# Exponentials on GpSimd at both ends of a two-branch attention kernel, and part of a softmax moved from VectorE to GpSimd

## The chip, the core and the metric

The kernel runs on one core of a Trainium2 chip. A core has TensorE (PE in the profile: matrix products into PSUM), ScalarE (ACT: activations), VectorE (DVE) and GpSimd (POOL) for elementwise work, and DMA queues, of which this kernel uses that of SyncE (SP). Each engine runs its own instructions in the order of the program and waits on semaphores for the others. The metric is the time of one execution on the device in microseconds; less is better.

## The reference, cut to what matters

```
x: 2048 x 512 (bf16)
g = sigmoid(sum(x * gate_w, -1))
a = attention of 32 heads of 16 over all 2048 keys, softmax(q k / 4) v, then @ A_wo
b = attention of 32 heads over 8 keys: positions s, s-2, ..., s-14, softmax(q k / 4) v, then @ B_wo
out = g * a + (1 - g) * b
```

Branch A is the full attention: 32 heads x 2048 x 2048 scores, each of which has to go through an exponential. Branch B is the local one: 8 scores for each position and head.

## The kernel before, in words

**Branch A.** The scores are made transposed, in units of 128 keys x 512 queries of one head. There are 2048 such units, in 32 periods of 64 (a period is four heads and one block of 512 queries). One matmul (`ring<-qt,kt_all` or `w<-qt,kt_all`) makes a unit in PSUM, one exponential turns it into a bf16 tile, and one matmul (`acc<-pT,vp_all` or `acc<-pd,vp_all`) multiplies it with the values and adds it to the accumulator of its period. The exponential can be had in two ways:

- on ScalarE, from a ring of PSUM banks, alternately three units and two units at a time (`act_stream`, `act_tail`; tile `pT`, lines `pT<-ring` of 128x1536 and 128x1024). Such a group is called a set below;
- on VectorE, one unit at a time from a PSUM buffer `w` (`dve_unit`): a cubic in the low 16 bits of the score, in four instructions (`ta<-w`, twice `ta<-ta,w`, then `pd<-ta,w`, which writes the bits of a bf16 number). `rider` and `solo` choose the units that take this way, at moments when the recorder below sees a free `w` and a free `pd`.

**Branch B.** It is done in 16 tiles of 128 positions (`b_proj`, `b_attn`), nearly all of it on GpSimd. For each tile GpSimd multiplies the shifted keys with the queries (`prod<-ksh,qb`, 8 instructions in two halves) and adds the products up (`prod<-prod`, `lg<-prod`). VectorE takes the maximum (`mx<-lg`), GpSimd subtracts it (`lg<-lg,mx`), ScalarE takes the exponential (`lg<-lg`), VectorE adds (`ssum<-lg`), takes the reciprocal, and multiplies by it and by 1 - g in one instruction (`lg<-lg,omg,ssum`). Then GpSimd multiplies with the shifted values (`prod<-vsh,lg`, 8 instructions) and adds (`prod<-prod`, `ob<-prod`, `obb<-ob,prod`); TensorE transposes the result (`w<-ident,obb`). Keys and values come through DRAM (`kv_scr`) by DMA into `ksh` (two buffers) and `vsh` (one buffer).

**Other work on GpSimd.** 12 times in the run, three instructions prepare packed queries of branch A (`mq<-qpk`, `mq<-mq,mbias`, `qpk<-mq,qpk`; called a packing job below).

**What sets the order.** The program is recorded by a planner (`Plan`): each piece of work is a generator that yields (engine, priority, duration, function). The planner keeps a clock of each engine, takes the ready piece with the lowest priority, and adds a fixed delay (`LAT`) before what comes next in the same generator. What it records is only an order for each engine; the chip then runs each engine's list in that order, with semaphores where data or buffers are shared. A piece that is late on the chip holds up everything that stands behind its readers on their engines. The planner also writes filler products (`acc<-ident,z`) into idle stretches of TensorE, so that TensorE stays busy.

All instructions go through one helper, so the profile gives nearly all of them the same line (L288); they are told apart by their tiles.

Of the kernel before, what the change touches and what calls it, by code (L numbers as in the profile page):

```python
# [10 lines left out]
ALU = mybir.AluOpType  # L11
# [21 lines left out]
A2 = 128.0 * 0.224337942 / 65536.0 ** 2  # L33
A1 = -128.0 * 0.303542182 / 65536.0
A0 = -128.0 * 0.000107113830


def _ap(base, dims):
# [9 lines left out]
class Plan:  # L48

    LAT = {"pe": 0.17, "act": 0.22, "dve": 0.12, "pool": 0.12, "sp": 0.08}

    def __init__(self, engines):
        self.free = {e: 0.0 for e in engines}
# [186 lines left out]
def kernel(  # L242
# [153 lines left out]
    P.resource("accS", 2)  # L396
    P.resource("kvs", 1)
    P.resource("mq", 1)
    MM = 0.22
    SW = 0.11  # L400
    VP = 0.60
# [4 lines left out]
    QRD = 2  # L406
    SOLO = 1
    TWICE = 0.60
    KRP = 4
    QRP = 3  # L410
    XARR = (5.0, 6.9, 8.8, 10.7)
# [182 lines left out]
    def kb_job(b, prio):  # L594
        for sc in range(NC):
            yield ("wait", ev_kpk[b][sc])
        st = {}
        cn = cneg[:, b, 0:1]
        yield ("dve", prio, 0.08, lambda: V.tensor_reduce(out=cn, in_=kmax_pk[:, b, :], axis=AX.X, op=ALU.max))
        yield ("dve", prio, 0.08, lambda: V.tensor_scalar(out=cn, in0=cn, scalar1=1e-20,  # L600
                                                         scalar2=-(1.0 + 2.0 ** -5), op0=ALU.max, op1=ALU.mult))

        def row():
            st["c"] = work.tile([128, QW], BF16, name="crow", tag="crow", bufs=1)
            V.tensor_copy(out=st["c"][:], in_=_ap(cn, [list(cn.ap[0]), [0, QW]]))
        yield ("dve", prio, VP, row)
        yield ("dve", prio, 0.08, lambda: V.reciprocal(out=cneg[:, b, 1:2], in_=cn))
        yield ("dve", prio, 0.08, lambda: V.tensor_tensor(out=mbias[:, b:b + 1], in0=cneg[:, b, 1:2], in1=m15[:],
                                                         op=ALU.mult))
        yield ("set", ev_kb[b])  # L610
        for sc in range(NC):
            yield ("sp", 0, 0.1, lambda sc=sc: SP.dma_start(out=scr_rows(k_scr[b], S, sc * QW, 1), in_=st["c"][:]))
        yield ("delay", 3.0)
        for g in range(2):
            i = 2 * (b + 1) + g
            yield ("sp", 0, 0.1, lambda i=i, g=g: SP.dma_start(out=kt_all[:, i, :],
                                                               in_=k_scr[b][128 * g:128 * (g + 1), :]))
            yield ("spawn", kt_landed(i))
# [6 lines left out]
    def qpk_job(c_, b, rel, prio):  # L625
        yield ("wait", rel)
        yield ("wait", ev_x[c_])
        yield ("wait", ev_kb[b])
        w = Bank()
        st = {}  # L630

        def pe(s):
            w.open(s, [128, QW])
            for c in range(DC):
                mm(w.t[:], wqr[:, c, 128 * (b + 1):128 * (b + 2)], xT[:, c, c_ * QW:(c_ + 1) * QW],
                   c == 0, c == DC - 1)
        yield ("pe", prio, 4 * MM + SW, pe, "w")

        def lin():
            st["q"] = work.tile([128, 2, QW], BF16, name="qpk", tag="qpk", bufs=2)  # L640
            V.tensor_scalar(out=st["q"][:, 0, :], in0=w.t[:], scalar1=QSC, scalar2=None, op0=ALU.mult)
        yield ("dve", prio, VP, lin)
        yield w.close()
        yield ("spawn", dma_job(lambda: SP.dma_start(out=scr_rows(q_scr[(c_, b)], QW, 0, 0), in_=st["q"][:, 0, :])))

        def relu():
            st["m"] = work.tile([128, QW], FP32, name="mq", tag="mq", bufs=1)
            G.tensor_scalar(out=st["m"][:], in0=st["q"][:, 0, :], scalar1=3.0e38, scalar2=0.0, op0=ALU.min, op1=ALU.max)
        yield ("acq", "mq", prio)
        yield ("pool", -5, 0.80, relu)  # L650
        yield ("pool", -5, 0.80, lambda: G.tensor_scalar(out=st["m"][:], in0=st["m"][:], scalar1=2.0,
                                                         scalar2=mbias[:, b:b + 1], op0=ALU.mult, op1=ALU.add))
        yield ("pool", -5, 1.22, lambda: G.tensor_tensor(out=st["q"][:, 1, :], in0=st["m"][:], in1=st["q"][:, 0, :],
                                                         op=ALU.subtract))
# [124 lines left out]
    DV_MIN = 12  # L779
    DV_END = 7  # L780
    flying = [0]
    njunk = [0]
    held_pv = [[] for _ in range(NP)]

# [52 lines left out]
    def pv_job(p, items, res, prio, act=True):  # L837
# [15 lines left out]
        def f():  # L853
# [17 lines left out]
            for e in list(pdq[p]):  # L871
                if e[0] <= now and (act_left[p] == 0 or cnt[e[2]] < most) and ready(ev_v[(i, e[1])], now):
                    pdq[p].remove(e)
                    cnt[e[2]] += 1
                    todo.append(e[1:4])
                    fin.append(("pd", e[4]))
            if act_left[p] == 0:
                for e in pdq[p]:
                    P.spawn(pv_job(p, [e[1:4]], ("pd", e[4]), 0.9, False), e[0])
                pdq[p].clear()  # L880
            seen = [0] * 4
            order = []
# [35 lines left out]
    def act_stream():  # L918
        while front[0] < NP:
# [32 lines left out]
            def f():  # L952
                shut = acc_open[0]
                twice = (shut is not None and not any(row_left[shut])
                         and P.have(P.now + dur) < TWICE * P.HAM)
                for _ in range(1 + twice):
                    for s_, (p_, t, j) in enumerate(units):
                        qk_mm(ring[:, s_, :], p_, t, j)
                more = MM * twice
                js = [u[2] for u in units]  # L960
                while len(js) < 4:
                    r = rider(js)
                    if r is None:
                        break
                    p_, t, j, s, ds = r
                    js.append(j)
                    wt = wtile(s, [128, QW])
                    qk_mm(wt[:], p_, t, j)
                    P.spawn(dve_unit(p_, t, j, s, ds, wt, ndve[0]), P.now + dur + more + P.LAT["pe"])
                    ndve[0] += 1  # L970
                return float(more)
            yield ("pe", 0, dur, f)
# [14 lines left out]
    def solo(t, end, most=SOLO):  # L987
# [7 lines left out]
        r = rider([], t)  # L995
        if r is None:
            return None
        p_, u, j, s, ds = r
        wt = wtile(s, [128, QW])
        qk_mm(wt[:], p_, u, j)  # L1000
        P.spawn(dve_unit(p_, u, j, s, ds, wt, ndve[0]), t + 0.33 + P.LAT["pe"])
        ndve[0] += 1
        nsolo[0] += 1
        return t
# [2 lines left out]
    def rider(js, now=None):  # L1007
        now = P.now if now is None else now
        for p in (front[0], front[0] + 1):
# [7 lines left out]
            j = max(opts, key=lambda j_: len(pend[p][j_]))  # L1017
            if flying[0] and any(x[6] and x[0] < 4.0 + 0.3 * min(front[0] + UR, 16.3) for x in P.ready["pe"]):
                return None
            if not P.free_at("w", now) or not P.free_at("pd", now):  # L1020
                return None
            act_left[p] -= 1
            act_due[p] -= 1
            flying[0] += 1
            return p, pend[p][j].pop(), j, P.take("w", now), P.take("pd", now)
        return None

    def dve_unit(p, t, j, s, ds, wt, n):
# [23 lines left out]
            yield ("spawn", pv_job(p, [(t, j, st["pd"][:])], ("pd", ds), 0.9, False))  # L1052
        else:
            now = yield ("now",)
            pdq[p].append((now, t, j, st["pd"][:], ds))

    otok_tiles = {}
    oT_tiles = {}
# [200 lines left out]
    def b_attn(t, rel, prio):  # L1259
# [19 lines left out]
        def loadk():  # L1279
            base = kv_scr[16 + t * 128:16 + (t + 1) * 128, :]  # L1280
            st["ksh"] = work.tile([128, W, D], BF16, name="ksh", tag="ksh", bufs=2)
            SP.dma_start(out=st["ksh"][:], in_=_ap(base, [[2 * D, 128], [-DIL * 2 * D, W], [1, D]]))
        yield ("sp", 0, 0.1, loadk)
        yield ("delay", 9.0)

# [52 lines left out]
            st["mx"] = work.tile([128, H], FP32, name="mx", tag="mx", bufs=2)  # L1338
            V.tensor_reduce(out=st["mx"][:], in_=lg[:], axis=AX.X, op=ALU.max)
        yield ("dve", prio, 0.33, mx)  # L1340
        yield ("pool", -4, 0.66, lambda: G.tensor_tensor(out=lg[:], in0=lg[:], in1=bc(st["mx"]), op=ALU.subtract))

        def ex():
            A.activation(out=lg[:], in_=lg[:], func=ACT.Exp)
        yield ("act", -1, 0.4, ex)

        def ssum():
            st["ss"] = work.tile([128, H], FP32, name="ssum", tag="ssum", bufs=2)
# [1 line left out]
        yield ("dve", prio, 0.33, ssum)  # L1350
        yield ("dve", prio, 0.27, lambda: V.reciprocal(out=st["ss"][:], in_=st["ss"][:]))

        def attn():
            V.scalar_tensor_tensor(out=lg[:], in0=lg[:], scalar=omg[:, t:t + 1], in1=bc(st["ss"]), op0=ALU.mult,
                                   op1=ALU.mult)
        yield ("dve", prio, 0.34, attn)
        yield ("delay", 1.0)

        def mul_v(hf, w_):
# [21 lines left out]
        for hf in range(2):  # L1381
# [5 lines left out]
            if hf == 0:  # L1387
                yield ("rel", "prod", 0)
        yield ("rel", "vsh", 0)
        yield ("set", _bmul[t])  # L1390

        def fin1():
# [2 lines left out]
        yield ("pool", gp - 0.5, 1.23, fin1)  # L1395
        yield ("rel", "prod", 0)
        yield ("rel", "ob", 0)
        w2 = Bank()
        cb, tl = t // TPC, t % TPC
        if tl == 0 and cb == 2:  # L1400
# [57 lines left out]
    v_group(0, 4, None, 3)  # L1458
    P.spawn(act_stream())
    P.spawn(g_job(GP))  # L1460
    def due(p):
        return 4.0 + 0.3 * min(p, 2 * NG)

# [32 lines left out]
    if CFG_DEBUG:  # L1496
# [2 lines left out]
        pickle.dump(LOG, open("/tmp/plan.pkl", "wb"))  # L1499
        left = {k: [(y[0], y[3].__name__) for y in v] for k, v in P.ready.items() if v}  # L1500
        left.update({k: [(y[0], y[3].__name__) for y in v] for k, v in P.reqs.items() if v})
        print("plan ends", {e: round(v, 1) for e, v in P.free.items()}, "junk", njunk[0], "dve units", ndve[0], "solo", nsolo[0], "sets", nset[0], left)
        if os.environ.get("PLANONLY"):
            raise SystemExit

# [34 lines left out]
```

## Time and profile before

| | |
|---|---|
| time, median of 5 runs | 880.31 us (877.41 to 881.37) |
| the execution that was profiled | 878.5 us, with a span of 876.7 us |
| ScalarE busy | 842.1 us (96% of the span), 829.7 us of it in 726 sets |
| VectorE busy | 768.1 us (88%), 234 units of branch A |
| TensorE busy | 766.9 us (87%) |
| GpSimd busy | 619.0 us (71%), first product of branch B at 112.2 us, last output at 800.0 us |
| DMA | 59.78 MB, mean 68 GB/s |

All numbers of instructions and durations are of the one profiled execution. In the profile's records two instructions that follow each other on ScalarE, VectorE or GpSimd can overlap by some hundredths or tenths of a microsecond, so the mean of one is a little more than what it adds to a row of them.

### The profile page before, as it was taken

How to read it: one execution, taken by the hardware profiler on the slowest of the kernel's cores; microseconds unless marked ns; L12 is line 12 of the kernel's file. 1: busy time of each engine (PE TensorE's matmuls, PEld its weight loads, DVE VectorE, ACT ScalarE, POOL GpSimd, SP SyncE). 2: the span in 40 equal slices, each digit the busy share in tenths (PEclk: the TensorE clock that was granted, in tenths of full speed). 3: DMA queues.
4: the chain of work that ended last, by engine and by line, in shares of the span. 5: the costliest groups of instructions: out<-in, count | busy, mean ns of one | idle time of the engine just before them, and what ended most of it. 6: DMA issues, size and time to landing. Idle time of an engine off the chain costs nothing.

```text
span 876.7 us, 15956 instructions
## 1 busy us (share of the span) xinstructions
PE 766.9 (87%) x6062; PEld 268.3 (31%) x6062; DVE 768.1 (88%) x1346; ACT 842.1 (96%) x758; POOL 619.0 (71%) x594
## 2 busy tenths in 40 slices
PE   8999989998898888888899999788888988898886
PEld 4332233333223233232333232222232222323222
DVE  4789889988989899989987878998998988989885
ACT  5999999999999999999999999999999999999995
POOL 2000283899797989898898989898989898955000
PEclk9899999999999999999999999999999999989999
DMA  8002213330414230321030403303031330200000
GB/s 289 2 1 96 73 32 116 113 121 22 144 46 146 70 112 19 114 63 46 12 117 30 133 27 119 103 8 108 1 92 43 96 105 7 67 1 7 1 1 25
DMA packets 55709, 59.78 MB, mean 68 GB/s; under 512 B 3648, under 2 KB 52288, under 8 KB 55632
## 3 DMA queue, kind: packets, MB, share of 16 engines
q1 hardware_dynamic: 54816, 58.50, 21.2%
q8 instruction: 47, 0.77, 0.4%
q10 hardware_dynamic: 816, 0.26, 0.1%
q14 instruction: 30, 0.25, 0.1%
HBM read 46.14 MB, written 12.62 MB: 67 GB/s over the span
## 4 chain that ended last, share of the span: by engine, by line
ACT 47%; PE 22%; issue 18%; DVE 12%; DMA 1%; SPq 0%; ACTq 0%
ACT pT L288 46%; PE w L288 8%; PE ring L288 7%; DVE ta L288 6%; PE acc L288 6%; DVE pd L288 1%; DVE lg L288 1%; DMA xr<-in_A_x_dram 1%; DVE accS L288 0%; PE last L288 0%; DVE ssum L288 0%; PE xt L288 0%; ACT lg L288 0%; DVE kvs L288 0%; DVE kpk L288 0%
## 5 line engine op out<-in xcount | busy, mean ns | idle before, releaser
L288 ACT ACTIVATE pT<-ring 128x1536 bf16<-128x1536 f32 x726 | 829.7, 1294 | 17.2 <-PE ring L288 8.4
L288 PE MATMUL ring<-qt,kt_all 32*128 32x512 bf16 x1878 | 293.1, 386 | 87.2 <-ACT pT L288 76.8
L288 DVE SCALAR_TENSOR_TENSOR ta<-ta,w 128x512 f32<-128x512 f32 x468 | 308.8, 681 | 5.0
L288 POOL TENSOR_TENSOR prod<-prod 128x512 f32<-128x512 f32 (+1 forms) x208 | 241.5, 1174 | 6.3
L288 PE MATMUL acc<-pT,vp_all 128*17 128x512 bf16 x1814 | 229.4, 388 | 0.1
L288 PEld LDWEIGHTS <-kt_all 32*128 32x128 bf16 x2112 | 105.0, 91 | 333.4 <-issue 319.0
L288 DVE TENSOR_SCALAR ta<-w 128x512 f32<-128x512 uint16 x234 | 158.1, 685 | 38.6 <-PE w L288 37.6
L288 PE MATMUL acc<-ident,z 128*32 128x512 bf16 (+6 forms) x750 | 168.0, 338 | 6.2 <-DVE accS L288 6.0
L288 DVE SCALAR_TENSOR_TENSOR pd<-ta,w 128x512 uint16<-128x512 f32 x234 | 156.7, 679 | 2.6
L288 POOL TENSOR_TENSOR prod<-ksh,qb 128x512 f32<-128x512 bf16 x128 | 145.6, 1163 | 10.9 <-DVE ta L288 8.8
L288 POOL TENSOR_TENSOR prod<-vsh,lg 128x512 f32<-128x512 bf16 x128 | 136.6, 1098 | 10.2 <-DVE lg L288 7.9
L288 PE MATMUL w<-qt,kt_all 32*128 32x512 bf16 x234 | 87.5, 387 | 1.2 <-DVE osb L288 0.6
L288 POOL TENSOR_SCALAR mq<-qpk 128x512 f32<-128x512 bf16 x12 | 7.4, 613 | 106.8 <-DVE qpk L288 106.8
L288 PE MATMUL acc<-pd,vp_all 128*17 128x512 bf16 x234 | 80.1, 386 | 0.2
L288 PEld LDWEIGHTS <-z 128*32 128x32 bf16 x774 | 51.7, 95 | 81.4 <-issue 63.5
L288 PEld LDWEIGHTS <-vp_all 128*17 128x17 bf16 x2048 | 44.5, 88 | 89.0 <-issue 86.5
L288 PE MATMUL w<-bw,xT 128*128 128x512 bf16 x192 | 49.6, 381 | 3.3 <-DVE pd L288 1.6
L288 PEld LDWEIGHTS <-xT 128*128 128x128 bf16 x512 | 31.4, 97 | 37.5 <-issue 24.0
L288 POOL TENSOR_TENSOR lg<-lg,mx 128x256 f32<-128x256 f32 x16 | 10.1, 629 | 37.2 <-DVE mx L288 37.1
L288 DVE CAST kvs<-w 128x512 bf16<-128x512 f32 x32 | 22.0, 687 | 11.7 <-PE w L288 11.6
L288 DVE COPY accS<-acc 128x512 f32<-128x512 f32 (+1 forms) x32 | 21.6, 675 | 1.8 <-ACT accS L288 1.5
L288 POOL TENSOR_TENSOR obb<-ob,prod 128x512 bf16<-128x512 f32 x16 | 20.3, 1271 | 1.3
(110 smaller groups left out, 438.5 us busy)
## 6 DMA issues: line engine op xcount, KB each, us to landing
ksh<-kv_scr SPq DMA_DIRECT2D x16, 1024.0 KB
vsh<-kv_scr SPq DMA_DIRECT2D x16, 1024.0 KB
kv_scr<-kvs SPq DMA_DIRECT2D x16, 256.0 KB
kt_all<-k_scr SPq DMA_DIRECT2D x6, 512.0 KB
q_scr<-qpk SPq DMA_DIRECT2D x24, 128.0 KB
qt<-q_scr SPq DMA_DIRECT2D x24, 128.0 KB
xr<-in_A_x_dram SPq DMA_DIRECT2D x4, 512.0 KB
out_dram<-osb SPq DMA_DIRECT2D x14, 128.0 KB
```

Of the source, the lines that this page charges most:

```text
L288: return chain_on(self._key, f(*a, **k))
```

## The change

- A third way to the exponential, on GpSimd (`pool_unit`): VectorE copies a unit's scores from PSUM into an SBUF tile `psc` (fp32, two buffers), and GpSimd does the cubic there, rewritten so that it takes six instructions with plain operands (three with one tensor operand, three with two). `psc` also holds the two intermediate tiles, and it lies in the buffer of `vsh`. So units go to GpSimd only before branch B begins (`ev_lent`) and after its last tile. The result, and the release of `psc`, are read 2.0 us after the planned end (`SLACK`); the transposes of `obb` are planned 2.0 us after its end as well.
- In branch B, the multiply by 1 - g and by the reciprocal leaves VectorE; GpSimd does it in two instructions, `ssum<-ssum,omg` (128x32) and `lg<-lg,ssum` (128x256).
- The planner's delay after a GpSimd piece goes from 0.12 to 0.02 us, and five of its planned durations are set anew.
- At most two units are on VectorE at a time when a new one is chosen; units chosen for GpSimd do not count in that.
- Where the recent TensorE work is under a threshold (`THIN`), one more filler product is written beside a set's products. The tile `crow` moves into the buffers of `kpk`.

```diff
-    LAT = {"pe": 0.17, "act": 0.22, "dve": 0.12, "pool": 0.12, "sp": 0.08}
+    LAT = {"pe": 0.17, "act": 0.22, "dve": 0.12, "pool": 0.02, "sp": 0.08}
...
-        yield ("pool", -5, 0.80, relu)
-        yield ("pool", -5, 0.80, lambda: G.tensor_scalar(...))          # mq<-mq,mbias
-        yield ("pool", -5, 1.22, lambda: G.tensor_tensor(...))          # qpk<-mq,qpk
+        yield ("pool", -5, 0.60, relu)
+        yield ("pool", -5, 0.66, lambda: G.tensor_scalar(...))
+        yield ("pool", -5, 1.12, lambda: G.tensor_tensor(...))
...
+                if (shut is not None and any(row_left[shut])
+                        and P.have(P.now + dur) < THIN * P.HAM):
+                    more += fill_pass(0.2134, P.now) + 0.01
...
-            if not P.free_at("w", now) or not P.free_at("pd", now):
+            if not P.free_at("w", now):
                 return None
+            hs = ds = None
+            if psc[0] is not None and rem(p) >= PMIN and P.free_at("psc", now):
+                hs = P.take("psc", now)
+                npool[0] += 1
+            else:
+                if not P.free_at("pd", now) or flying[0] > 1:
+                    return None
+                flying[0] += 1
+                ds = P.take("pd", now)
...
+    def pool_unit(p, t, j, s, hs, wt, n):
+        sc, y, z = psc[0][:, hs, :], psc[0][:, 2, :], psc[0][:, 3, :]
+        yield ("dve", 39, VP, lambda: V.tensor_copy(out=sc, in_=wt[:]))
+        yield ("rel", "w", s)
+        yield ("acq", "py", n)
+        lo = sc.bitcast(U16).rearrange("p (n two) -> p n two", two=2)[:, :, 0]
+        yield ("pool", 0, 0.66, lambda: G.tensor_scalar(out=y, in0=lo, scalar1=YA, scalar2=YA * YS, ...))
+        yield ("pool", 0, 1.30, lambda: G.tensor_tensor(out=z, in0=y, in1=y, op=ALU.mult))
+        yield ("pool", 0, 0.66, lambda: G.tensor_scalar(out=z, in0=z, scalar1=1.0, scalar2=YB, ...))
+        yield ("pool", 0, 1.30, lambda: G.tensor_tensor(out=z, in0=z, in1=y, op=ALU.mult))
+        yield ("pool", 0, 1.30, lambda: G.tensor_tensor(out=z, in0=z, in1=sc, op=ALU.add))
+        yield ("spawn", later(SLACK, ("rel", "psc", hs)))
+        ds = yield ("acq", "pp", n)
+        yield ("pool", 0, 0.66, fin)                                    # pd<-psc, uint16
+        yield ("rel", "py", 0)
+        yield ("delay", SLACK)
...
-        yield ("pool", -4, 0.66, lambda: G.tensor_tensor(out=lg[:], in0=lg[:], in1=bc(st["mx"]), op=ALU.subtract))
+        yield ("pool", -4, 0.60, lambda: G.tensor_tensor(out=lg[:], in0=lg[:], in1=bc(st["mx"]), op=ALU.subtract))
-        yield ("act", -1, 0.4, ex)
+        yield ("act", -1, 0.31, ex)
...
-            V.scalar_tensor_tensor(out=lg[:], in0=lg[:], scalar=omg[:, t:t + 1], in1=bc(st["ss"]), ...)
-        yield ("dve", prio, 0.34, attn)
+        yield ("pool", -4, 0.12, lambda: G.tensor_scalar(out=st["ss"][:], in0=st["ss"][:], scalar1=omg[:, t:t + 1], ...))
+        yield ("pool", -4, 0.60, lambda: G.tensor_tensor(out=lg[:], in0=lg[:], in1=bc(st["ss"]), op=ALU.mult))
...
         yield ("rel", "ob", 0)
+        yield ("delay", SLACK)
```

More of the change, by code (lines that the diff above doesn't have):

```diff
@@ L35 @@
 A0 = -128.0 * 0.000107113830
+YS = A2 / (3.0 * A3)
+YA = A3 ** (1.0 / 3.0)
+YB = (A1 - 3.0 * A3 * YS * YS) / YA
+YC = A0 - A3 * YS ** 3 - (A1 - 3.0 * A3 * YS * YS) * YS
 def _ap(base, dims):
@@ L398 @@
     P.resource("mq", 1)
+    P.resource("psc", 2)
+    P.resource("py", 1)
+    P.resource("pp", 2)
     MM = 0.22
@@ L408 @@
     TWICE = 0.60
+    THIN = 0.40
     KRP = 4
@@ L603, in row @@
         def row():
-            st["c"] = work.tile([128, QW], BF16, name="crow", tag="crow", bufs=1)
+            st["c"] = work.tile([128, QW], BF16, name="crow", tag="kpk", bufs=2)
             V.tensor_copy(out=st["c"][:], in_=_ap(cn, [list(cn.ap[0]), [0, QW]]))
@@ L649, in qpk_job @@
         yield ("acq", "mq", prio)
-        yield ("pool", -5, 0.80, relu)
-        yield ("pool", -5, 0.80, lambda: G.tensor_scalar(out=st["m"][:], in0=st["m"][:], scalar1=2.0,
+        yield ("pool", -5, 0.60, relu)
+        yield ("pool", -5, 0.66, lambda: G.tensor_scalar(out=st["m"][:], in0=st["m"][:], scalar1=2.0,
                                                          scalar2=mbias[:, b:b + 1], op0=ALU.mult, op1=ALU.add))
-        yield ("pool", -5, 1.22, lambda: G.tensor_tensor(out=st["q"][:, 1, :], in0=st["m"][:], in1=st["q"][:, 0, :],
+        yield ("pool", -5, 1.12, lambda: G.tensor_tensor(out=st["q"][:, 1, :], in0=st["m"][:], in1=st["q"][:, 0, :],
                                                          op=ALU.subtract))
@@ L781 @@
     flying = [0]
+    psc = [None]
+    psc_end = [None]
+    pusers = [0]
+    npool = [0]
+    PMIN = 22
+    SLACK = 2.0
+    ev_lent = Event()
     njunk = [0]
@@ L875, in f @@
                     todo.append(e[1:4])
-                    fin.append(("pd", e[4]))
+                    fin.append(e[4])
             if act_left[p] == 0:
                 for e in pdq[p]:
-                    P.spawn(pv_job(p, [e[1:4]], ("pd", e[4]), 0.9, False), e[0])
+                    P.spawn(pv_job(p, [e[1:4]], e[4], 0.9, False), e[0])
                 pdq[p].clear()
@@ L964, in f @@
                         break
-                    p_, t, j, s, ds = r
+                    p_, t, j, s, ds, hs = r
                     js.append(j)
@@ L968, in f @@
                     qk_mm(wt[:], p_, t, j)
-                    P.spawn(dve_unit(p_, t, j, s, ds, wt, ndve[0]), P.now + dur + more + P.LAT["pe"])
+                    P.spawn(vec_unit(p_, t, j, s, ds, hs, wt, ndve[0]), P.now + dur + more + P.LAT["pe"])
                     ndve[0] += 1
@@ L997, in solo @@
             return None
-        p_, u, j, s, ds = r
+        p_, u, j, s, ds, hs = r
         wt = wtile(s, [128, QW])
         qk_mm(wt[:], p_, u, j)
-        P.spawn(dve_unit(p_, u, j, s, ds, wt, ndve[0]), t + 0.33 + P.LAT["pe"])
+        P.spawn(vec_unit(p_, u, j, s, ds, hs, wt, ndve[0]), t + 0.33 + P.LAT["pe"])
         ndve[0] += 1
@@ L1019, in rider @@
                 return None
-            if not P.free_at("w", now) or not P.free_at("pd", now):
+            if not P.free_at("w", now):
                 return None
+            hs = ds = None
[7 more added lines that the diff above has]
+                ds = P.take("pd", now)
             act_left[p] -= 1
             act_due[p] -= 1
-            flying[0] += 1
-            return p, pend[p][j].pop(), j, P.take("w", now), P.take("pd", now)
+            return p, pend[p][j].pop(), j, P.take("w", now), ds, hs
         return None
@@ L1054, in dve_unit, with vec_unit, fin @@
             now = yield ("now",)
-            pdq[p].append((now, t, j, st["pd"][:], ds))
+            pdq[p].append((now, t, j, st["pd"][:], ("pd", ds)))
+    def vec_unit(p, t, j, s, ds, hs, wt, n):
+        return dve_unit(p, t, j, s, ds, wt, n) if hs is None else pool_unit(p, t, j, s, hs, wt, n)
+    def pool_unit(p, t, j, s, hs, wt, n):
+        sc, y, z = psc[0][:, hs, :], psc[0][:, 2, :], psc[0][:, 3, :]
+        st = {}
+        pusers[0] += 1
+        yield ("dve", 39, VP, lambda: V.tensor_copy(out=sc, in_=wt[:]))
+        yield ("rel", "w", s)
+        yield ("acq", "py", n)
+        lo = sc.bitcast(U16).rearrange("p (n two) -> p n two", two=2)[:, :, 0]
+        yield ("pool", 0, 0.66, lambda: G.tensor_scalar(out=y, in0=lo, scalar1=YA, scalar2=YA * YS, op0=ALU.mult,
+                                                        op1=ALU.add))
+        yield ("pool", 0, 1.30, lambda: G.tensor_tensor(out=z, in0=y, in1=y, op=ALU.mult))
+        yield ("pool", 0, 0.66, lambda: G.tensor_scalar(out=z, in0=z, scalar1=1.0, scalar2=YB, op0=ALU.mult,
+                                                        op1=ALU.add))
+        yield ("pool", 0, 1.30, lambda: G.tensor_tensor(out=z, in0=z, in1=y, op=ALU.mult))
+        yield ("pool", 0, 1.30, lambda: G.tensor_tensor(out=z, in0=z, in1=sc, op=ALU.add))
+        yield ("spawn", later(SLACK, ("rel", "psc", hs)))
+        ds = yield ("acq", "pp", n)
+        def fin():
+            st["pd"] = work.tile([128, QW], BF16, name="pd", tag=f"pp{ds}", bufs=1)
+            G.tensor_scalar(out=st["pd"][:].bitcast(U16), in0=z, scalar1=1.0, scalar2=YC - VOFF / 2.0, op0=ALU.mult,
+                            op1=ALU.add)
+        yield ("pool", 0, 0.66, fin)
+        yield ("rel", "py", 0)
+        pusers[0] -= 1
+        if pusers[0] == 0 and psc_end[0] is not None:
+            yield ("set", psc_end[0])
+        yield ("delay", SLACK)
+        if act_left[p] == 0:
+            yield ("spawn", pv_job(p, [(t, j, st["pd"][:])], ("pp", ds), 0.9, False))
+        else:
+            now = yield ("now",)
+            pdq[p].append((now, t, j, st["pd"][:], ("pp", ds)))
@@ L1057, with later, psc_job @@
+    def later(d, what):
+        yield ("delay", d)
+        yield what
+    def psc_job(stop):
+        yield ("acq", "vsh", 99)
+        psc[0] = work.tile([128, 4, QW], FP32, name="psc", tag="vsh", bufs=1)
+        if stop is None:
+            return
+        psc_end[0] = Event()
+        yield ("wait", stop)
+        psc[0] = None
+        if pusers[0]:
+            yield ("wait", psc_end[0])
+        psc_end[0] = None
+        yield ("rel", "vsh", 0)
     otok_tiles = {}
@@ L1282, in loadk @@
             SP.dma_start(out=st["ksh"][:], in_=_ap(base, [[2 * D, 128], [-DIL * 2 * D, W], [1, D]]))
+        if t == 0:
+            yield ("set", ev_lent)
         yield ("sp", 0, 0.1, loadk)
@@ L1351, in b_attn @@
         yield ("dve", prio, 0.27, lambda: V.reciprocal(out=st["ss"][:], in_=st["ss"][:]))
-        def attn():
-            V.scalar_tensor_tensor(out=lg[:], in0=lg[:], scalar=omg[:, t:t + 1], in1=bc(st["ss"]), op0=ALU.mult,
-                                   op1=ALU.mult)
-        yield ("dve", prio, 0.34, attn)
+        yield ("pool", -4, 0.12, lambda: G.tensor_scalar(out=st["ss"][:], in0=st["ss"][:], scalar1=omg[:, t:t + 1],
+                                                         scalar2=None, op0=ALU.mult))
+        yield ("pool", -4, 0.60, lambda: G.tensor_tensor(out=lg[:], in0=lg[:], in1=bc(st["ss"]), op=ALU.mult))
         yield ("delay", 1.0)
@@ L1389, in b_attn @@
         yield ("rel", "vsh", 0)
+        if t == NT - 1:
+            yield ("spawn", psc_job(None))
         yield ("set", _bmul[t])
@@ L1460 @@
     P.spawn(g_job(GP))
+    P.spawn(psc_job(ev_lent), 16.0)
     def due(p):
@@ L1501 @@
         left.update({k: [(y[0], y[3].__name__) for y in v] for k, v in P.reqs.items() if v})
-        print("plan ends", {e: round(v, 1) for e, v in P.free.items()}, "junk", njunk[0], "dve units", ndve[0], "solo", nsolo[0], "sets", nset[0], left)
+        print("plan ends", {e: round(v, 1) for e, v in P.free.items()}, "junk", njunk[0], "dve units", ndve[0], "solo", nsolo[0], "pool", npool[0], "sets", nset[0], left)
         if os.environ.get("PLANONLY"):
```

## The prediction, before the changed kernel ran

> **What bounds the kernel now.** First the page's busy shares, then the groups by form, then the waits.
>
> ```profile
> PE 766.9 (87%) x6062; PEld 268.3 (31%) x6062; DVE 768.1 (88%) x1346; ACT 842.1 (96%) x758; POOL 619.0 (71%) x594
> POOL 2000283899797989898898989898989898955000
> ```
> ```profile
> L288 ACT ACTIVATE pT<-ring 128x1536 bf16<-128x1536 f32 x363 | 546.4, 1505 | 12.2 <-PE ring L288 4.9 <-PE w L288 4.2 <-PE acc L288 0.3
> L288 ACT ACTIVATE pT<-ring 128x1024 bf16<-128x1024 f32 x362 | 392.1, 1083 | 5.0 <-PE ring L288 3.5 <-PE w L288 0.8
> L288 POOL TENSOR_TENSOR prod<-prod 128x512 f32<-128x512 f32 x176 | 221.9, 1276 | 3.8
> ...
> L288 DVE SCALAR_TENSOR_TENSOR lg<-lg,omg,ssum 128x256 f32<-128x256 f32 x16 | 14.2, 887 | 0.1
> ```
> ```profile
> POOL mq L288 <- DVE qpk L288: 106.8, 12, 76.2
> ...
> POOL lg L288 <- DVE mx L288: 37.1, 12, 11.2
> ```
>
> ScalarE is the bound: its sets have 17 us of idle time before them in 877. GpSimd is empty for the first tenth and the last tenth (the row of digits), and in between, where branch B runs, it is nearly full; there it mostly waits for VectorE's maximum.
>
> The chain gives ScalarE's true pace: four alternating sets in 4.44 us, 1.11 us each.
>
> ```profile
> 116.61 4.44 ACT pT L288 x4
> ```
>
> Branch B's stage is measured between the first and last exponential of `lg` (144.0 to 780.1), and one tile of it on GpSimd from one `lg<-lg,mx` to the next (322.27 to 361.45):
>
> ```profile
> L288 ACT ACTIVATE lg<-lg x16: 409/454/658, 144.0 to 780.1; 128x256 f32<-128x256 f32 x16
> ```
> ```profile
> 322.27 0.63 POOL L288 TENSOR_TENSOR lg<-lg,mx 128x256 f32<-128x256 f32 x1 [1.83 <-DVE mx L288]
> ...
> 343.85 3.84 POOL L288 TENSOR_TENSOR prod<-prod 128x512 f32<-128x512 f32 x3
> 347.77 1.27 POOL L288 TENSOR_TENSOR obb<-ob,prod 128x512 bf16<-128x512 f32 x1
> 349.12 4.50 POOL L288 TENSOR_TENSOR prod<-ksh,qb 128x512 f32<-128x512 bf16 x4
> ...
> 361.45 0.63 POOL L288 TENSOR_TENSOR lg<-lg,mx 128x256 f32<-128x256 f32 x1 [1.64 <-DVE mx L288]
> ```
>
> The tile takes 39.18 us, 1.64 of it waiting: 37.5 us of work. Six tiles without a packing job give 37.4 to 37.6. Where the next instruction needs the result of the one before, 0.08 us lies between them (343.85 + 3.84 to 347.77).
>
> **Part 1: units leave ScalarE.** Counted in the two programs' orders, 24 units go to GpSimd, VectorE's fall from 234 to 225, ScalarE's from 1814 to 1799: 720 sets instead of 726. Six sets at 1.11 are **-6.7 us**. This gain stands only if ScalarE never waits more than before.
>
> **Part 2: VectorE.** It loses nine units (9 x (0.685 + 2 x 0.681 + 0.679) = 24.5 us) and 16 multiplies (14.2), and gains 24 copies at the 0.687 of `kvs<-w` (16.5): 22 us less. ScalarE hardly waits for VectorE now, so I take this at zero; at best it is a few of the 5 us before sets that a product into `w` ended: credit up to 3. The `crow` copies can wait for the `k_scr` writes from their new buffers, three times; one such transfer is hidden behind other VectorE work, else at most about 2 us each.
>
> The multiply is a special case. With two SBUF inputs of 256 elements it took 469 to 1520 ns (mean 887), and the maximum over as many elements 407 to 415. The Trainium skill, "SBUF — State Buffer", section "Who interferes with whom", says that a VectorE instruction with two SBUF inputs contends with GpSimd instructions that read SBUF, and that a reduction never does; that fits the spread. By that rule its removal frees GpSimd's reads too, some tenths per tile, which would lower the sum below by up to 16 x 0.4 us; the sum goes without it.
>
> **Part 3: the 24 GpSimd units.** No row has the operation on GpSimd. The nearest are `prod<-prod` with two operands (1.27) and `mq<-mq,mbias` with one (8.6/12 = 0.71), each followed by the 0.08 gap: 3 x 1.35 + 3 x 0.79 = 6.4 us a unit. The low end is 3 x 1.16 + 3 x 0.61 = 5.3 (`prod<-ksh,qb`, `mq<-qpk`, no gap); the high end 6 x 1.35 = 8.1, if reading every other 16 bits costs as much as a second operand. Twelve units stand ahead of branch B: 77 us, with two packing jobs (2 x 2.5) 82. GpSimd was idle from 11.5 to 112.2 but for these two. Scores exist from 19 us on, so the twelve fit if they start by 25; the order has B's first exponential four sets earlier than before, so nothing is to spare, and I take zero. Twelve stand behind the last output: 77 us, where 720 sets less some 643 leave 77 sets or 90 us. They are planned at 6.0 us each (3 x 0.68 + 3 x 1.32); 12 x 0.4 = 4.8 us late less the 2.0 of `SLACK`, up to 2.8 us on TensorE's products behind them if all come back to back. That goes into the range.
>
> **Part 4: branch B gets less time.** This decides. With the delay of 0.02 instead of 0.12 us after each of some 34 instructions, the order puts a tile 3 us closer to the next. In the order of ScalarE the first and last exponential of `lg` were 544 sets apart and are now 523. Before, 636.1/544 = 1.169 us a set, all stalls of ScalarE included. The tight part is from tile 3 to tile 12 (counted from 0), with 297 sets for nine tiles: 297 x 1.169 = 347 us. GpSimd's need there: nine times 37.5, plus the new multiply (0.63 from `lg<-lg,mx`, and 0.08), plus the small one. No row is near 128x32: it costs between 0.1 (the 0.10 of the one-element memsets) and 0.43 (`lg<-prod`, 128x128); I take 0.15, as it is a quarter of that width, and 0.08. So 9 x 38.45 = 346, and five packing jobs stand in this part, 5 x 2.5 = 12.5: **358.5 us**. Short by 11.5. GpSimd enters with the wait that a tile had in hand, about 2.5 us (37.1/12 is 3.1). **+9.0 us.** The loose parts (112 sets, 131 us, for 120 of work; 114 sets, 133 us, for 123) can't give it back: once ScalarE has waited, that time is gone. Who waits: VectorE at `mx`, and ScalarE at `lg<-lg`, which has no slack and is followed in its queue by the next set; behind `mx` stand the VectorE units and evacuations that free `w` for TensorE.
>
> At the multiply a rule speaks against the change: the Trainium skill, "GPSIMD Engine Reference", section "4.1 Engine selection", gives elementwise work to VectorE because GpSimd is about twice as slow with two inputs. This trace has 1.27 against 0.68 us for 512 elements, but VectorE's multiply was itself no faster than GpSimd's subtraction (0.89, 0.63). Twice 0.41 in place of 0.63 would add 9 x 0.2 = 1.8 us.
>
> **Sum.** -6.7 + 9.0 = +2.3 us: 880.8 against the profiled execution's own 878.5. That one lies 1.8 under the median; beside the 880.31 the time is **882.6**. The filler products add five weight loads, nothing.
>
> **The rivals.**
>
> *Faster: GpSimd holds its pace.* If it enters the tight part with the whole spare of the loose one (131 - 120 = 11 us), the shortage is covered and -6.7 stands: 873.6, or to 872 with VectorE's credit. For it: the products of a next tile stand ahead of `lg<-lg,mx`, so some work is done in advance. Against it: at every `lg<-lg,mx` GpSimd stops until VectorE comes to `mx` (37.1 us of such waits), so a lead does not pass a tile. The point: a lead of 9 us or more at tile 3 decides for it, one under 5 against.
>
> *Much slower: the front units overrun.* At the high end, 8.1 us, the twelve need 20 us more, branch B begins that much late, and ScalarE is held at its first `lg<-lg`: 882.6 + 20 = 903; at 6.9 us a unit, 889. For it: no row shows a 16-bit read with a stride on GpSimd, and there is no spare. Against: on VectorE the same read costs nothing (0.685 against 0.681).
>
> *The stalls of TensorE's clock differ.* The clock dips in the first tenth and in 750 to 800 us; a dip more or less, or the new filler, may move 2 us and hide the rest: within 0.3%.
>
> **How the numbers follow.** GpSimd bound 0.55; its own range is 878 (credit of 3, head start of 4) to 888 (small multiply at 0.43, tail 2.8). GpSimd keeping pace 0.25. Front overrun 0.15. Clock alone 0.05. A measurement here can tell about 0.3%, 2.6 us, from no change. The first case gives 0.04 faster, 0.26 same, 0.25 slower; so faster 0.29, same 0.31, slower 0.40. For 8 in 10 the range runs from 872.5, which holds the faster case, to 889.
>
> **What would show it.** Right: GpSimd's waits for `mx` in the tight part fall from 2 to 3 us a tile to nearly none; ScalarE's `lg<-lg` and VectorE's `mx` wait for POOL where no such row is now; the chain runs through POOL's `prod` there; first to last `lg<-lg` takes about 620 us, not 611. Wrong: waits for `mx` stay and the stage takes 611 us (first rival), or the first `prod<-ksh,qb` starts after 115 us and the wait at ScalarE's first `lg<-lg` is over 3 us (second). A wait of TensorE for `pd` from GpSimd at the end would show the tail at fault.

## The result and the profile after

| | before | after |
|---|---|---|
| time, median | 880.15 us (47 runs) | 883.27 us (26 runs, 878.95 to 886.97) |
| ratio | | 1.0041 (95% interval 1.0030 to 1.0052) |
| profiled execution, its span | 878.5, 876.7 us | 886.07, 884.3 us |

The change makes the kernel 0.4% slower. The prediction was 882.6 us. The profiled execution of after lies 2.8 us above its median and that of before 1.7 below, so the two spans differ by more (7.6) than the medians (3.1).

The page: busy shares, the row of GpSimd in slices, and the shares of the chain that ended last.

```profile
PE 776.1 (88%) x6065; PEld 270.7 (31%) x6065; DVE 753.7 (85%) x1318; ACT 836.5 (95%) x752; POOL 761.2 (86%) x770
...
POOL 2586797989899999999999999999798979879663
...
POOL 37%; ACT 28%; PE 15%; issue 14%; DVE 4%; DMA 2%; SPq 0%; POOLq 0%; ACTq 0%
POOL prod L292 30%; ACT pT L292 27%; PE w L292 5%; PE ring L292 5%; PE acc L292 5%; POOL lg L292 2%; DVE ta L292 2%; POOL obb L292 1%; POOL ob L292 1%; DMA vsh<-kv_scr 1%; POOL psc L292 1%; POOL qpk L292 1%; POOL mq L292 1%; PE last L292 1%; DMA xr<-in_A_x_dram 1%
```

The empty ends of GpSimd's row are filled, and in the middle it has a run of nines. GpSimd was not in the chain before; now it holds 37% of it, most of it branch B's products.

The waits of after. The first column waits for the second: us in total, times, longest.

```profile
POOL psc L292 <- DVE psc L292: 44.1, 10, 11.7
...
POOL ssum L292 <- DVE ssum L292: 12.2, 5, 2.6
DVE mx L292 <- POOL lg L292: 8.7, 8, 1.6
...
POOL lg L292 <- DVE mx L292: 8.2, 8, 1.7
...
ACT lg L292 <- POOL lg L292: 5.3, 5, 1.7
...
POOL ssum L292 <- ACT pT L292: 4.8, 3, 2.6
```

The direction has turned. GpSimd waited 37.1 us for VectorE's maximum, now 8.2; and VectorE waits at `mx` and ScalarE at `lg<-lg` for GpSimd, which did not occur before. GpSimd also waits at its new small multiply (`ssum`, 12.2 + 4.8 us). Nearly all of its waits in branch B lie outside the tight part, tiles 3 to 12: inside it, up to the wait that ends it, they are 0.3 us for `mx` and 0.2 at `ssum`. All five waits of ScalarE at `lg<-lg` lie inside.

One tile of the tight part on GpSimd, from one `lg<-lg,mx` to the next, shows the new pieces between the old ones:

```profile
315.87 0.63 POOL L292 TENSOR_TENSOR lg<-lg,mx 128x256 f32<-128x256 f32 x1
...
319.93 0.35 POOL L292 TENSOR_SCALAR ssum<-ssum,omg 128x32 f32<-128x32 f32 x1
...
321.46 0.62 POOL L292 TENSOR_TENSOR lg<-lg,ssum 128x256 f32<-128x256 f32 x1
...
353.22 0.63 POOL L292 TENSOR_TENSOR lg<-lg,mx 128x256 f32<-128x256 f32 x1 [0.29 <-DVE mx L292]
```

37.35 us with 0.29 of waiting, against 39.18 with 1.64 in the tile shown of before; but this one has seven key products, and that one eight. The other tiles of the tight part without a packing job and without a gap take 38.1 to 38.3 us. Over the nine tiles 3 to 12 the gaps of more than 0.15 us in GpSimd's row sum to 2.2 us, all told, 1.7 of them at the very end, before the `lg<-lg,mx` of tile 12.

### The profile page after: what moved, and what is told of

Its sections match the earlier page's. It is cut to its first block, busy times and chain, and to the rows that moved or that the text cites. A ratio compares the mean times of both kernels' runs of the same rounds, so it can differ in the third digit from the quotient of the medians.

```text
span 884.3 us, 16171 instructions
## 1 busy us (share of the span) xinstructions
PE 776.1 (88%) x6065; PEld 270.7 (31%) x6065; DVE 753.7 (85%) x1318; ACT 836.5 (95%) x752; POOL 761.2 (86%) x770
## 4 chain that ended last, share of the span: by engine, by line
POOL 37%; ACT 28%; PE 15%; issue 14%; DVE 4%; DMA 2%; SPq 0%; POOLq 0%; ACTq 0%
POOL prod L292 30%; ACT pT L292 27%; PE w L292 5%; PE ring L292 5%; PE acc L292 5%; POOL lg L292 2%; DVE ta L292 2%; POOL obb L292 1%; POOL ob L292 1%; DMA vsh<-kv_scr 1%; POOL psc L292 1%; POOL qpk L292 1%; POOL mq L292 1%; PE last L292 1%; DMA xr<-in_A_x_dram 1%
## 5 line engine op out<-in xcount | busy, mean ns | idle before, releaser
L292 DVE SCALAR_TENSOR_TENSOR ta<-ta,w 128x512 f32<-128x512 f32 x450 | 299.3, 682 | 5.9
L292 DVE TENSOR_SCALAR ta<-w 128x512 f32<-128x512 uint16 x225 | 152.6, 685 | 36.2 <-PE w L292 34.2
L292 PE MATMUL acc<-ident,z 128*32 128x512 bf16 (+3 forms) x751 | 173.1, 345 | 4.3 <-DVE accS L292 3.3
L292 DVE SCALAR_TENSOR_TENSOR pd<-ta,w 128x512 uint16<-128x512 f32 x225 | 151.4, 679 | 2.6
L292 PE MATMUL w<-qt,kt_all 32*128 32x512 bf16 x249 | 93.4, 386 | 2.0 <-DVE pd L292 1.9
L292 POOL TENSOR_TENSOR psc<-psc 128x512 f32<-128x512 f32 x72 | 85.9, 1193 | 5.7
L292 PE MATMUL acc<-pd,vp_all 128*17 128x512 bf16 x249 | 81.9, 393 | 0.0
L292 POOL TENSOR_SCALAR psc<-psc 128x512 f32<-128x512 uint16 (+1 forms) x48 | 29.7, 619 | 47.2 <-DVE psc L292 44.1
L292 PE MATMUL w<-identf,accS 128*128 128x128 f32 x124 | 22.1, 305 | 0.2
```

The lines of the kernel that those rows point to most:

```text
L292: return chain_on(self._key, f(*a, **k))
```

## The experiments

Theory 1: the tight order of branch B makes GpSimd the bound, and ScalarE pays for it. The rivals: the new work itself costs (units, multiply), or TensorE's clock does. All were timed in five rounds against the kernel before; the ratios compare best.

| run | edit | median us | ratio (95% interval) |
|---|---|---|---|
| the change | | 883.27 | 1.0041 (1.0030 to 1.0052) |
| e1_light | same order, lighter sums on GpSimd | 870.25 | 0.9889 (0.9863 to 0.9916) |
| e2_lat12 | delay 0.12 | 873.33 | 0.9928 (0.9903 to 0.9954) |
| e3_lat06 | delay 0.06 | 870.23 | 0.9886 (0.9860 to 0.9912) |
| e4_dve_mul | multiply on VectorE, delay 0.02 | 893.19 | 1.0147 (1.0108 to 1.0186) |
| e5_before_lat02 | the kernel before, delay 0.02 | 883.68 | 1.0039 (1.0020 to 1.0059) |
| e6_lat06_nounits | delay 0.06, no units on GpSimd | 876.44 | 0.9949 (0.9929 to 0.9970) |
| e7_lat06_dve | delay 0.06, multiply on VectorE | 880.68 | 1.0027 (1.0000 to 1.0054) |
| e8_lat07 | delay 0.07 | 873.65 | 0.9925 (0.9896 to 0.9953) |
| e9_dve_narrow | as e7, multiply on 32 of 256 elements | 877.78 | 0.9961 (0.9940 to 0.9981) |
| e10_slack0 | delay 0.06, SLACK 0.1 | 872.27 | 0.9913 (0.9883 to 0.9943) |
| e11_measured | delay and durations as measured | 873.39 | 0.9913 (0.9882 to 0.9944) |

**e1_light.**

```diff
+                m = 2 if n == 8 else n
-                G.tensor_tensor(out=pv_[:, w0:w1, :, 0:n], in0=pv_[:, w0:w1, :, 0:n], in1=pv_[:, w0:w1, :, n:2 * n],
+                G.tensor_tensor(out=pv_[:, w0:w1, :, 0:m], in0=pv_[:, w0:w1, :, 0:m], in1=pv_[:, w0:w1, :, n:n + m],
```

> The changed kernel with its order kept, and GpSimd's work in branch B made lighter: the four widest sums of the key products of a tile add 2 of 8 columns, so that part of branch B's sums is left out. Theory 1 (GpSimd is the bound in tiles 3 to 12): each of the four goes from 1.27 to some 0.4 us, 3.5 us less a tile, 31 us less in nine tiles, far more than the shortage of 11.5; ScalarE is the bound again and the 6 sets less pay in full: about 874 us against 880 of the kernel before, and waits of GpSimd for mx come back. Rival (TensorE's clock, or the units at the two ends, cost the time): still about 883.

Measured 870.25. The order of all engines is that of the change; only GpSimd's four sums a tile are shorter, so a part of branch B's sums is left out. The whole loss goes, and nearly 4 us more than expected. The same nine tiles as a stage, of after and then of this run. The numbers are the window, its length, the busy time of TensorE, of its weight loads, of VectorE, ScalarE and GpSimd (with the number of their records), the clock that TensorE was granted (1.00 is full), the DMA share and GB/s:

```profile
271.99:628.30 356.31, 311.52 (x2364) 105.05 (x2364) 313.47 (x542) 341.61 (x307) 345.64 (x339) 0.98 0.25 76
```
```profile
266.92:614.17 347.25, 306.61 (x2368) 105.03 (x2368) 313.47 (x543) 341.78 (x308) 319.36 (x339) 1.00 0.25 79
```

ScalarE's busy time is the same, 341.6 and 341.8 us. The stage is 9.1 us shorter with 26 us less of GpSimd work: that is ScalarE's waiting. Of it, 5.3 us were waits for GpSimd at `lg<-lg` (now none), and ScalarE's waits for TensorE's products fell from 8.2 to 4.5 us. GpSimd's wait for `mx` is back:

```profile
POOL lg L292 <- DVE mx L292: 36.1, 16, 4.5
```

**e2_lat12, e3_lat06, e8_lat07.** One number of the planner.

```diff
-    LAT = {"pe": 0.17, "act": 0.22, "dve": 0.12, "pool": 0.02, "sp": 0.08}
+    LAT = {"pe": 0.17, "act": 0.22, "dve": 0.12, "pool": 0.12, "sp": 0.08}      # e2; 0.06 in e3, 0.07 in e8
```

> The changed kernel with the planner's delay after GpSimd put back to 0.12 us; the multiply and the units stay on GpSimd (21 units now, 721 sets). First to last exponential of lg are 542 sets apart instead of 523, and nine tiles have 322 sets, 376 us, for some 357 us of GpSimd. Theory 1: GpSimd waits for mx again, 2 us a tile, and 5 sets less at 1.11 us pay: 874 to 876 us. Rival (the new work itself costs, wherever it stands): 880 or more.

> The changed kernel with a delay of 0.06 us after GpSimd (22 units, 721 sets; first to last exponential 529 sets apart; tiles 3 to 12 have 305 sets, 356.5 us, for 354 to 357 us of GpSimd work). Theory 1: just at the edge, GpSimd nearly without waits and ScalarE waiting for it by 0 to 2 us in all: 875 to 878 us. Rival: 880 or more, as in the run with 0.12.

> The changed kernel with a delay of 0.07 us (721 sets; tiles 3 to 12 have 310 sets, 362 us, for 357 us of GpSimd). Theory 1: past the edge GpSimd is no bound, and the time is that of the version with 0.06 within 1.5 us: 869 to 872. If each hundredth of the delay counted by itself, it would lie halfway to the 873.3 of 0.12 or further: 871 to 873.

All three beat both kernels: 873.3, 870.2 and 873.7. The first two are 1 and 5 us better than theory 1 said, the third 2 us worse, and above both of the ranges that it was to decide between; against 883.3 the theory's sign is clear, the rival (880 or more) is out. Between 0.06, 0.07 and 0.12 the intervals overlap, so which delay is best is not settled. The chain of e3_lat06 has no GpSimd in it:

```profile
ACT 54%; PE 21%; issue 21%; DVE 4%; ACTq 0%
```

**e5_before_lat02.** The same line in the kernel before, 0.12 to 0.02, and nothing else.

> The kernel before with one edit, the planner's delay after GpSimd at 0.02 instead of 0.12 us; no units on GpSimd, the multiply on VectorE (725 sets). Tiles 3 to 12 get 293 sets, 342.5 us, for 9 x 37.5 + 12.5 = 350 us of GpSimd. Theory 1 (the tight order is the harm, whatever the new work): 5 us or more slower, 884 to 892 us. Rival (the added GpSimd work is the harm): 879 to 880, as the kernel before.

Measured 883.68, +0.39%: just under what theory 1 gave (884 to 892), and as much as the whole change costs. At a clock of 0.986 its three runs took 883.2 to 884.3 us, the four of the kernel before 878.3 to 879.9. With no new work on GpSimd at all, the tight order alone puts it into the chain, and brings the waits of VectorE and ScalarE for it:

```profile
ACT 33%; POOL 21%; PE 17%; issue 14%; DVE 13%; DMA 2%; SPq 0%; POOLq 0%; ACTq 0%; DVEq 0%
```
```profile
DVE mx L288 <- POOL lg L288: 4.7, 6, 1.8
...
ACT lg L288 <- POOL lg L288: 2.7, 5, 1.2
```

GpSimd itself waited here for the transfers of `ksh` and `vsh` as well (8.6 and 9.1 us, three times in all), which it did not in the kernel before; what these add to the loss is not separated.

**e4_dve_mul.**

```diff
-        yield ("pool", -4, 0.12, lambda: G.tensor_scalar(out=st["ss"][:], ...))
-        yield ("pool", -4, 0.60, lambda: G.tensor_tensor(out=lg[:], in0=lg[:], in1=bc(st["ss"]), op=ALU.mult))
+        yield ("dve", prio, 0.34, attn)
```

> The changed kernel with the multiply of branch B back on VectorE (one instruction, as before); delay 0.02 and the units on GpSimd stay (25 units, 721 sets). The order then packs branch B as tightly: 521 sets from first to last exponential, 292 sets or 341 us for nine tiles, for 338 us of bare work and five packing jobs (12.5). Theory 1: GpSimd is short by as much as before, and the time stays at 882 to 886 us. Rival (the multiply moved to GpSimd is what costs, some 1.0 us a tile): 16 us of work less on GpSimd, and about 874 to 876.

Measured 893.19: the rival is out, but theory 1 missed by 7 us as well. In this order the multiply costs more on VectorE than on GpSimd, 10 us by the medians. GpSimd now waits for it:

```profile
POOL prod L292 <- DVE lg L292: 15.8, 4, 4.5
```

**e6_lat06_nounits.** `PMIN = 999` in the version of e3.

> The version with a delay of 0.06 us, but without any unit on GpSimd (725 sets instead of 721; the multiply stays on GpSimd; tiles 3 to 12 have 309 sets, 361 us, no shortage). Theory 1: the units save ScalarE 4 sets of 1.11 us against this one, so it takes 4 to 5 us more than the version with 0.06: 874 to 876 us. Rival (the units cost at both ends, by their copies on VectorE and by waits, about what they save): 870 to 871.

Measured 876.44, just above theory 1's range; the rival is out. The 22 units are worth 0.6% (0.9949 against 0.9886), 5.5 us for four sets. Even without them this version is 0.5%, 4.5 us, faster than the kernel before, with one set less (1.1 us). That the rest comes from the multiply is not shown: this version's median clock was higher (0.988 against 0.985), and at a clock of 0.986 its three runs took 876.5 to 878.2 us and the four of the kernel before 878.3 to 879.9. Nor is it free of GpSimd, which holds 18% of its chain.

**e7_lat06_dve.** The edit of e4 in the version of e3.

> The version with a delay of 0.06 us and the multiply back on VectorE (722 sets; tiles 3 to 12 have 301 sets, 352 us, for 350 us of GpSimd). Theory 2 (the multiply is better on GpSimd, because VectorE's has two SBUF inputs, takes 0.7 to 0.9 us where 0.34 is planned, and its delay is carried by all that stands behind it): 874 to 880 us. Rival (the multiply on GpSimd costs about 1 us a tile where GpSimd is at its limit, so without it the version is as fast or faster): 868 to 871.

Measured 880.68, just above theory 2's range; the rival is out. Taking the multiply back to VectorE costs 1.4%, 12 us by the ratios (10.5 by the medians, and 9 at a clock of 0.988, where three runs took 878.8 to 881.3 and two of e3_lat06 871.1 and 872.4). It reaches ScalarE as waits for TensorE's products, here and then in e3_lat06:

```profile
ACT pT L292 <- PE ring L292: 12.4, 16, 2.9
ACT pT L292 <- PE w L292: 7.9, 12, 2.3
```
```profile
ACT pT L292 <- PE ring L292: 7.9, 15, 2.9
...
ACT pT L292 <- PE w L292: 4.1, 10, 0.9
```

**e9_dve_narrow.** Is it the multiply's own time? The version of e7, with most of branch B's weights left unscaled.

```diff
-            V.scalar_tensor_tensor(out=lg[:], in0=lg[:], scalar=omg[:, t:t + 1], in1=bc(st["ss"]), op0=ALU.mult, op1=ALU.mult)
+            V.scalar_tensor_tensor(out=lg[:, 0:4, :], in0=lg[:, 0:4, :], scalar=omg[:, t:t + 1],
+                                   in1=_ap(r[:], [list(r[:].ap[0]), [1, 4], [0, W]]), op0=ALU.mult, op1=ALU.mult)
```

> The version with a delay of 0.06 us and the multiply on VectorE, its order kept; the multiply covers 32 of 256 elements, so most of branch B's weights stay undivided and unscaled. Theory 2a (the multiply's own time on VectorE, 0.47 to 1.5 us where 0.34 is planned, is what makes that version 10 us slower than the one with the multiply on GpSimd): its row falls to 0.2 to 0.3 us, and the time to 871 to 875. Theory 2b (it is its place: GpSimd's value products wait for VectorE to come to it, and the order then packs the rest more tightly): the waits of prod for lg stay and the time stays at 878 to 881.

Measured 877.78, between the two ranges: by the ratios 5.8 of the 12 us go, by the medians 2.9 of the 10.5. The row of the multiply in e7 and then here (minimum, median and maximum in ns):

```profile
L292 DVE SCALAR_TENSOR_TENSOR lg<-lg,omg,ssum x16: 469/744/1507, 142.9 to 766.3; 128x256 f32<-128x256 f32 x16
```
```profile
L292 DVE SCALAR_TENSOR_TENSOR lg<-lg,omg,ssum x16: 234/610/1287, 143.2 to 763.6; 128x32 f32<-128x32 f32 x16
```

With an eighth of the elements the shortest falls by half, but the median stays at 610 ns. So most of this instruction's time is not its elements. 2a expected a row of 0.2 to 0.3, which did not come, so it was not really tested. The sign of 2b did come: GpSimd waits before the first value product of the same six tiles, 20.5 us in e7 and 20.3 here, only that the list of waits now puts 17.7 of them (4.4 in e7) down to others than `lg`. But e3_lat06 has waits at this place too, 12.3 us before its small multiply and 2.9 before the products, so they need not be what costs the 12 us. What is left, the wait inside the multiply or its place in VectorE's queue, is not separated.

**e10_slack0 and e11_measured.** `SLACK = 0.1` in the version of e3; and a delay of 0.08 with these durations:

```diff
-            yield ("pool", gp, 1.22, add_k(8, 2, 4))
-            yield ("pool", gp, 1.22, add_k(4, 0, 4))
+            yield ("pool", gp, 1.27, add_k(8, 2, 4))
+            yield ("pool", gp, 1.27, add_k(4, 0, 4))
...
-        yield ("pool", -4, 0.12, lambda: G.tensor_scalar(out=st["ss"][:], ...))
+        yield ("pool", -4, 0.33, lambda: G.tensor_scalar(out=st["ss"][:], ...))
```

> The version with a delay of 0.06 us, but with SLACK at 0.1 instead of 2.0 us, so that GpSimd's units and the transposes of obb are read right at their planned end (720 sets, tiles 3 to 12 have 307 sets). If readers on TensorE then wait for a GpSimd that runs some us late: 873 to 878 us, and rows of TensorE waiting for POOL. If what waits is VectorE at mx and ScalarE at lg, which have no slack in either version: 869 to 871.

> The changed kernel with a delay of 0.08 us after GpSimd, as the trace has it between dependent instructions, and with GpSimd's planned durations in branch B set so that duration and delay together give the measured distance from start to start (1.11 for a key product, 1.06 for a value product, 1.34 for a dependent sum, 0.33 for the small multiply). 721 sets; tiles 3 to 12 have 305 sets, 356.5 us, for 357 of work. Theory 1 (an order that gives GpSimd just what it takes keeps the gain): 869 to 872 us, like the version with 0.06; if the edge needs a margin: 873 or more.

872.27, between the two ranges of e10, and 873.39, in the second of e11, both with a ratio of 0.9913. Each interval overlaps that of e3, so neither settles anything about 2 us. In e10 the only waits of another engine for GpSimd that the list of waits shows are TensorE's weight loads, 0.9 us for `prod` and 0.4 for `obb`; VectorE's `mx` has none. So reading GpSimd's results at their planned end costs little once the order leaves it enough time.

## Why the prediction was right, and where its terms were off

**The mechanism** was as described: GpSimd short of time from tile 3 to tile 12, VectorE and ScalarE waiting for it. First to last `lg<-lg` was to take about 620 us:

```profile
L292 ACT ACTIVATE lg<-lg x16: 416/437/522, 142.2 to 762.2; 128x256 f32<-128x256 f32 x16
```

762.2 - 142.2 = 620.0. The order was to allow the tight part 347 us, and in e1_light, without the shortage, it took 347.25; the shortage was put at 9.0 us, and the stage of the change is 9.1 us longer. That close an agreement is partly luck: GpSimd was to work 358.5 us with 2.5 in hand, 356.0, and it worked 354.1 and stood for 2.2. e5 shows that the delay of 0.02 us, part 4 of the prediction, is enough for the harm without the new work, and e2, e3 and e8 that the harm goes when the delay is longer.

**The medians and the clock.** By the medians, e1_light gains 880.15 - 870.25 = 9.9 us where the prediction had 6.7 + 0 for the sets and VectorE, and the change loses 883.27 - 870.25 = 13.0 from there where it had 9.0. Both are some 3 to 4 us larger, and nearly cancel: +3.1 measured, +2.3 predicted. What is larger goes with the clock granted to TensorE. Over all runs its median is 0.985 in the kernel before, 0.992 in e1_light and 0.979 with the change, and within each of the three the time rises by about 4 to 5 us when it is lower by 0.01. Runs at the same clock:

| clock | before, us | e1_light, us | the change, us |
|---|---|---|---|
| 0.986 | 878.26, 878.28, 878.35, 879.93 | 873.31 | 881.20, 882.23 |
| 0.989 | 877.85, 877.93 | 871.58 | 880.66 |

There the first step is -5 and -6 us and the second +8 and +9. Straight lines through all runs of each version, read at 0.985, give -6.4 and +8.0 (an estimate). So at one clock the two terms of the sum stand about as predicted, and what the medians have beyond them was the prediction's last rival, the stalls of the clock, which it put at 2 us.

The profiled pair shows the same. Beside the 9.1 us of the nine tiles, its windows ahead of the first and behind the last `lg<-lg` differ by 4.0 and 3.3 us, with nearly the same work and another clock (the third number from the end), the change first and then e1_light:

```profile
0.00:142.00 142.00, 128.96 (x1111) 50.00 (x1111) 102.68 (x189) 126.58 (x116) 94.80 (x111) 0.95 0.29 93
762.00:884.30 122.30, 101.00 (x779) 34.29 (x777) 100.16 (x171) 108.86 (x99) 83.48 (x90) 0.94 0.05 14
```
```profile
0.00:138.00 138.00, 123.67 (x1108) 50.37 (x1108) 103.03 (x188) 125.69 (x116) 91.57 (x111) 1.00 0.30 96
747.00:866.00 119.00, 95.66 (x779) 34.02 (x777) 100.06 (x171) 108.22 (x99) 83.50 (x90) 1.00 0.04 12
```

Inside the tight part the clock differs too (0.98 against 1.00). There the change has three stretches at half clock, from about 319 to 326, 514 to 517 and 589 to 596 us, where e1_light has one. The first two begin 2 to 3 us after waits of ScalarE for GpSimd (0.9 and 1.7 us, ended at 316.5 and 511.0); the third begins together with such a wait (1.05 us) and so hardly comes from it, and the two shorter waits (0.8 and 0.7 us) have none near. The kernel before, where ScalarE never waits for GpSimd, has such stretches as well (28 to 35, 93 to 97, 369 to 373 and 765 to 776 us). Whether the change lowers the clock or the executions differ by chance stays open.

**Part 2, VectorE at zero,** fits the sum at one clock, where e1_light gains 5 to 6.4 us for six sets at 1.11. No run takes the multiply off VectorE in the order of before, and none has the bounded number of units on VectorE, the new filler or `crow` alone. What the step did not see is what the multiply holds up when it stays in a tighter order (9 to 12 us in e7). It was weighed by its busy time and by who waits in the trace of before. The rule that spoke against the move, which would have made it 0.82 us on GpSimd, did not hold here: `lg<-lg,ssum` took 0.62 to 0.65 us.

**Part 3.** A unit on GpSimd was taken at 6.4 us. Its rows:

```profile
L292 POOL TENSOR_TENSOR psc<-psc 128x512 f32<-128x512 f32 x72 | 85.9, 1193 | 5.7
...
L292 POOL TENSOR_SCALAR psc<-psc 128x512 f32<-128x512 f32 x24 | 14.9, 620 | 2.1
L292 POOL TENSOR_SCALAR psc<-psc 128x512 f32<-128x512 uint16 x24 | 14.8, 618 | 45.1 <-DVE psc L292 44.1
L292 POOL TENSOR_SCALAR pd<-psc 128x512 uint16<-128x512 f32 x24 | 14.8, 617 | 2.1
```

130.4 us for 24, 5.4 each, and under 0.5 of gaps: near the low end of 5.3. The strided 16-bit read costs nothing extra (618 against 620), so the second rival had no ground. Of its sign one half came: the first key product did start after 115, at 120.8 us. The other did not: the first `lg<-lg` came at 142.2, no later than before, and no wait of ScalarE for GpSimd was over 1.7.

**Part 4's small multiply** takes 361 ns, nearer to the upper end (0.43) than to the 0.15 taken. **The first rival**, a lead at tile 3 that covers the shortage, did not come: GpSimd stood in each of the first three tiles (3.6, 3.0 and 2.5 us) and went into tile 3 with nothing in hand beyond one such wait, as argued. **The tail** shows no wait of TensorE for a `pd` of GpSimd; `SLACK` was not the matter (e10). Two slips changed nothing: the first rival with VectorE's full credit of 3 would be 870.6, not 872, and the tiles of before without any part of a packing job are five, not six.

## What to carry to other kernels

A planner's per-instruction delay is a budget: 0.1 us times 34 instructions was 3 us a tile, and taking it out of the order made a side engine a bound even without any added work (e5). Work for an idle engine should be costed on the stretch where that engine is busiest, and a moved instruction also on the queue that it leaves: here, with the delay at 0.06, putting one 0.9 us multiply back cost 1.4%, where the units were worth 0.6%. When a large rearrangement moves the time little, a run with the same order and less work on the suspected engine separates its gain from its loss at once, if the runs are also compared at the same clock.

## What the runs showed of the hardware that was not expected

A VectorE multiply with two SBUF inputs of 32 elements took 234 to 1287 ns with a median of 610 in e9, beside a GpSimd that was busy most of the time, and one of 256 elements 469 to 1507 with 744 in e7; a maximum over 256 elements took 361 to 421 in e9. The Trainium skill, "SBUF — State Buffer", section "Who interferes with whom", says that the first kind contends with GpSimd instructions that read SBUF and a reduction does not, and calls this contention an exclusive lock. The long times with so few elements agree with that, though no run here had GpSimd idle for comparison.

GpSimd took 361 ns for 128x32 with one tensor operand and 618 for 128x512: sixteen times the elements for 1.7 times the time.
